# Two interleaved layers, a spectral filter and a long convolution: the last eight units of the convolution's kernel are made in the second part

## The chip, the cores and the metric

One core of one Trainium2 chip runs the whole program. The metric is device time in microseconds (us) of one execution; smaller is better. Engines are called PE (TensorE), DVE (VectorE), ACT (ScalarE), POOL (GpSimd) and SP (SyncE, which here only issues DMAs).

## The reference

Four residual steps on x of 2048 x 512 values: layer A, layer B, layer A, layer B, each on a layer norm of x.

```python
def _A_ref(x, w_r, w_i):                     # S, D = 2048, 512
    X = rfft2(x) * (w_r + 1j * w_i)
    return irfft2(X, s=(S, D))

def _B_ref(u, ...):                          # D = 512 channels, N = 128 states, L = 2048
    P = exp(dt * A * l)                      # complex, D x N x L
    K = einsum("dn,dnl,dn->dl", C, P, dt * B).real
    y = irfft(rfft(u, 2 * L) * rfft(K, 2 * L))[:L]
    return y + u * Dskip

x = x + _A_ref(layernorm(x), ...)
x = x + _B_ref(layernorm(x), ...)
x = x + _A_ref(layernorm(x), ...)
x = x + _B_ref(layernorm(x), ...)
```

Both layers B use the same K, which does not depend on x.

## The kernel before

Transforms are matmuls with cosine and sine tables in several steps. x stays in SBUF as 128 partitions x 16 rows (`s2`) x 512 columns.

**The kernel K** is made in 32 units (`unit_k`) of 16 channels. Four units are a block `b`, eight units a quarter `q` of the channels. For a block, `load_k` loads factors by DMA, and six steps of `exp_k` make magnitudes: two factor matmuls into a PSUM pair (L1194) and one exponential on ACT (L1210) into a buffer `M`. A unit then does this:

- PE: two factor matmuls, the phases, into a PSUM pair `p` (L1194)
- ACT: `c` = phases plus a constant that rounds them (L1224)
- DVE: `s`, the phase's remainder, from `c` and `p` (L1226), and its absolute value into `c` (L1227)
- ACT: sine of `c`, the cosine part (L1229), and of `s` (L1230, written to PSUM `p`)
- DVE: the imaginary half of `E` = sine times magnitude (L1237 and L1238, which read PSUM `p` and SBUF `M`)
- POOL: the real half of `E` = `c` times magnitude (L1241 and L1242)
- PE: 64 small matmuls of `E` (L1254), and DVE two copies of their sums into `KS` (L1265)

After eight units `store_k` sends `KS` to DRAM (`kd`, L1274), and `turn_k` loads it back (L1285), turns it on PE (L812) and sends it, by way of ACT copies (L1301), to DRAM `yk`. For the first half of the channels (units 0 to 15) `spectra_k` makes spectra from `yk` in the first part and stores them in `khat`.

**Layer A** (`forward_a`, `first_a`, `group_a`, `inv_a`) goes in 16 rows, 16 groups of frequencies and 16 inverse rows. After its inverse, `inv_a` adds the result to x on DVE (L792, L794).

**Layer B** works on two halves `e` of the columns. `norm_b` normalises a row of x (for the first layer on DVE, L554; for the second on ACT, L552). `turn_x` turns 32 columns of it (PE L828, and a DVE transpose, L830). Columns 128 to 255 go another way: `forward_b` (PE L812, ACT copies, DMA to DRAM `yd`) and `place_b` (DMA back, L859). Then eight groups `group_b` for each half: PE spectrum of rows (L881), DVE times the spectra of K (L951), POOL sums (L958), PE back (L968), ACT copies (L973). The second half's groups of the first layer load `yk` (L929) and make their spectra of K there; all others load `khat` (L940). `inv_b` (L1019) and `back_b` bring the result to x.

**The order** is made when the program is built: each step is a generator of pieces, a class `Clock` keeps modelled times of engines, buffers and dependences, and a list scheduler emits the piece of the lowest rank among those that are ready. The engines then run that order, each its own instructions strictly one after another. Matmuls at L413 fill PE's modelled idle time. There are two such lists, run one after the other: the **first part** (loads, all of K but the last quarter's turn, the first layer A, the first norms), and the **second part** (the last quarter's turn, first layer B, second layer A, second layer B). No piece of the second part stands ahead of one of the first on any engine. I call the place where they meet the seam. Buffers are rings cut from three big tiles (`wk`, `Y`, `Ya`) anew for each part; PSUM is split in banks by kind, the `a` kind having three pairs in the first part and four in the second.

Of the kernel before, what the change touches and what calls it, by code (L numbers as in the profile page):

```python
# [53 lines left out]
WORK = 16896  # L54
# [143 lines left out]
class Clock:  # L198
# [4 lines left out]
    def __init__(self, net, last=None):  # L203
# [3 lines left out]
        self.pools, self.lands = [], []  # L207
# [231 lines left out]
class Net:  # L439
    def __init__(self, tc, io, ctx):  # L440
# [324 lines left out]
    def inv_a(self, r, s2, st):  # L765
# [21 lines left out]
        nc.tensor.matmul(q, self.RaT, Y4, start=True, stop=True)  # L787
        self.drop(Y4)
# [25 lines left out]
    def norm_b(self, r, s2, st):  # L814

        k = (id(st), s2 // 4, s2 // 2 % 2) if r else (id(st), s2 // 4)
        yield "ACT" if NORMS[2 * r + 1] else "DVE", self.after(k), self.emitted(("group", 1), 16 * r), self.emitted(("inverse", 0), 16)
        self.norm(s2, st, slice(0, 512), self.xn[:, s2])
        self.mark("normed", r, s2 // 4)

    def turn_x(self, r, e, i):

        yield "PE p:a", *(self.after(("normed", r, b), 4) for b in range(4)), self.emitted(("turned", r), 4), self.emitted(("mult", r), PACE[r] * i * e)
        p = self.psum("a")
        o = 256 * e + 32 * i
        for w in range(2):
            rows = slice(64 * w, 64 * w + 64)
            self.nc.tensor.matmul(p[:, 512 * w:512 * w + 512], self.Rf[rows, :], self.xn[rows, :, o:o + 32], start=True, stop=True)  # L828
# [4 lines left out]
    def forward_b(self, r, b):  # L833

        kind = "f" if r else "a"
        ring = "iy" if r else f"t{1 + b // 2}"
# [5 lines left out]
        self.turn_b(self.xn[:, 4 * b:4 * b + 4, 128:256], ps)  # L842
# [137 lines left out]
    def back_b(self, r, e, b):  # L980
# [5 lines left out]
        yield "SP io", self.after(("grouped", r, e), 8), self.emitted(("rows", r, 1), 8)  # L986
# [26 lines left out]
    def inv_b(self, r, e, i):  # L1013
# [3 lines left out]
        yield "DVE wo", self.after(("grouped", r, e), 8), self.emitted(("rows", r, 1), 8), self.emitted(("mult", r), 8 + LATE[r] * (i - first) if not e else 0)  # L1017
# [45 lines left out]
    def load_h(self):  # L1063
        self.oh = self.ring["oh"][0].bitcast(BF)[:96]
# [114 lines left out]
    def load_k(self, b):  # L1179
# [334 lines left out]
```

## Time and profile before

| | before |
|---|---|
| median of 3 runs | 748.66 us (745.71 to 748.88) |
| the profiled execution | 748.11 us |
| its span | 746.3 us |
| PE busy | 624.4 us (84%) |
| DVE busy | 556.4 us (75%) |
| ACT busy | 405.2 us (54%) |
| POOL busy | 279.3 us (37%) |
| DMA | 121.52 MB, mean 163 GB/s |

A profile's row names the line of the kernel, the engine, the operation, output and inputs by the program's names, and the shape. The span runs from the first instruction to the last. An idle time is put down to what ended it. "Busy" PE includes the filling matmuls of L413.

### The profile page before, as it was taken

The page shows a single profiled execution, that of the slowest core. Times are in us where ns is not written, and L with a number is a line of the kernel's source. Part 1 is how long each engine was busy: PE and PEld are TensorE (multiplying, and loading weights), DVE is VectorE, ACT ScalarE, POOL GpSimd, SP SyncE. Part 2 cuts the span into 40 slices and gives each one's busy share as a digit, 9 for nine tenths or more (in the row PEclk, how much of TensorE's full clock was granted, in tenths as well). Part 3 has the DMA queues.
Part 4 walks back from the last instruction along what each step waited for, and adds up shares of the span by engine and source line. Part 5 has one row for each costly group of instructions (what it writes and reads, how often), then busy time and mean ns, then how long its engine had stood idle before and what let it go on. Part 6 is the DMA issues. An engine that isn't in the chain of part 4 may idle for free. (4 is left out here: it accounts for less than half of the span.)

```text
span 746.3 us, 19649 instructions
## 1 busy us (share of the span) xinstructions
PE 624.4 (84%) x8138; PEld 390.1 (52%) x8138; DVE 556.4 (75%) x923; ACT 405.2 (54%) x654; POOL 279.3 (37%) x275
## 2 busy tenths in 40 slices
PE   3799888888989888878688899889887799898883
PEld 3778566556755434344333446477766544444241
DVE  5977578657685877589569899786798488798664
ACT  5677889887788886784223431176544145322220
POOL 4283255534353533051035452075444100056440
PEclk9999999999999999989899999899999999999997
DMA  9433412642432973544997766400658000578967
GB/s 334 138 106 106 133 51 86 164 128 84 115 114 62 310 203 94 183 142 113 310 320 237 247 208 227 163 1 1 219 194 274 2 2 1 198 244 260 351 184 206
DMA packets 109785, 121.52 MB, mean 163 GB/s; under 512 B 5916, under 2 KB 90912, under 8 KB 109568
## 3 DMA queue, kind: packets, MB, share of 16 engines
q1 hardware_dynamic: 67760, 90.90, 38.3%
q10 hardware_dynamic: 41936, 29.37, 12.4%
q8 instruction: 64, 1.05, 0.6%
q14 instruction: 25, 0.20, 0.1%
HBM read 80.53 MB, written 39.71 MB: 161 GB/s over the span
## 5 line engine op out<-in xcount | busy, mean ns | idle before, releaser
L958 POOL TENSOR_TENSOR apart<-wk 128x512 f32<-128x512 f32 x64 | 79.8, 1274 | 167.7 <-DVE wk L951 154.8
L1241 POOL TENSOR_TENSOR Y<-wk,Y 128x1024 f32<-128x1024 f32 x32 | 64.8, 2023 | 113.4 <-issue 68.0
L951 DVE TENSOR_TENSOR wk<-ps,wk 128x1024 f32<-128x1024 f32 x64 | 74.5, 1220 | 15.0 <-PE ps L881 5.3
L973 ACT COPY Y<-ps 128x512 f32<-128x512 f32 x64 | 34.4, 589 | 92.9 <-PE ps L968 82.9
L413 PEld LDWEIGHTS ps<-cRa,cRb 128*128 128x128 f32 x550 | 64.3, 193 | 18.4 <-issue 13.1
L413 PE MATMUL ps<-cRa,cRb 128*128 128x128 f32 x550 | 69.3, 281 | 3.3 <-DMA cRb<-in_cRb_dram 3.3
L779 PE MATMUL ps<-cDaT,apart 128*32 128x256 f32 x256 | 60.8, 388 | 4.5 <-DVE x L794 4.5
L1226 DVE SCALAR_TENSOR_TENSOR wk<-wk,ps 128x1024 f32<-128x1024 f32 x32 | 38.9, 1215 | 16.5 <-ACT wk L1224 16.4
L830 DVE STREAM_TRANSPOSE Y<-ps 128x1024 f32<-128x1024 f32 x24 | 44.4, 1930 | 6.3 <-PE ps L828 6.2
L968 PE MATMUL ps<-apart,wk 32*64 32x256 f32 x1024 | 43.1, 398 | 6.6 <-POOL apart L958 5.7
L1210 ACT ACTIVATE Y<-ps 128x1024 f32<-128x1024 f32 x48 | 46.0, 1028 | 4.8 <-PE ps L1194 4.1
L1194 PE MATMUL ps<-wk,Y 96*128 96x512 bf16 x128 | 40.5, 394 | 9.2 <-ACT Y L1210 4.6
L597 PE MATMUL ps<-cRa,wk 128*128 128x256 f32 x128 | 35.6, 403 | 14.9 <-POOL wk L579 13.6
L1254 PEld LDWEIGHTS ps<-Y 128*32 128x32 f32 x2048 | 34.8, 121 | 25.0 <-issue 19.2
L1254 PE MATMUL ps<-Y 128*32 128x64 f32 x2048 | 39.8, 237 | 9.6 <-ACT wk L783 3.5
L579 POOL TENSOR_TENSOR wk<-wk 128x256 f32<-128x256 f32 x32 | 26.2, 819 | 55.3 <-ACT wk L552 26.5
L1237 DVE TENSOR_TENSOR Y<-ps,Y 128x1024 f32<-128x1024 f32 x32 | 39.0, 1218 | 9.2 <-ACT ps L1230 9.2
L779 PEld LDWEIGHTS ps<-cDaT,apart 128*32 128x32 f32 x256 | 26.7, 111 | 34.9 <-DVE x L794 8.1
L881 PE MATMUL ps<-Y,wk 64*32 64x256 f32 x1024 | 36.3, 392 | 9.4 <-ACT Y L973 4.5
L1229 ACT ACTIVATE wk<-wk,quarter 128x1024 f32<-128x1024 f32 x32 | 36.7, 1147 | 13.2 <-DVE wk L1227 11.2
L1224 ACT ACTIVATE wk<-ps,magic 128x1024 f32<-128x1024 f32 x32 | 35.4, 1123 | 9.7 <-PE ps L1194 3.6
L1019 DVE STREAM_TRANSPOSE Ya<-Y 128x1024 f32<-128x1024 f32 x16 | 34.1, 2154 | 7.3 <-ACT Y L973 7.3
(205 smaller groups left out, 1512.4 us busy)
## 6 DMA issues: line engine op xcount, KB each, us to landing
wk<-khat SPq DMA_DIRECT2D x24, 512.0 KB
yk<-wk ACTq DMA_DIRECT2D x32, 256.0 KB
Ya<-vd SPq DMA_DIRECT2D x16, 512.0 KB
Y<-in_W_dram SPq DMA_DIRECT2D x12, 515.0 KB
x<-in_cPa_dram SPq DMA_DIRECT2D x16, 384.0 KB
Y<-in_cGa_dram SPq DMA_DIRECT2D x12, 384.0 KB
x<-in_W_dram SPq DMA_DIRECT2D x16, 258.0 KB
x<-in_A_x_dram SPq DMA_DIRECT2D x8, 512.0 KB
```

Of the source, the lines that this page charges most:

```text
L413: self.net.nc.tensor.matmul(bank[:, :128], self.net.Rb, self.net.Ra[:, 1], start=True, stop=True)
L779: nc.tensor.matmul(p[32 * i:32 * i + 32, o:o + 256], self.folded(r, i)[:, b, s2].rearrange("p g m -> p (g m)"), self.DaT[:, b, :], start=b ...
L830: self.nc.vector.transpose(self.place[e][:, :, 32 * i:32 * i + 32].rearrange("p k d -> p d k"), p.rearrange("p (w s d) -> p d s w", w=2, s ...
L951: nc.vector.tensor_tensor(t[c], x, kh[:, :, ::-1, :] if c else kh, op=OP.mult)
L958: nc.gpsimd.tensor_tensor(Z[:, :, c], t[0][:, :, c], t[1][:, :, c], op=op)
L968: nc.tensor.matmul(v[j][64 * a:64 * a + 64, h], gi[o:o + 32, j, 4 + 2 * c:6 + 2 * c, :].rearrange("p a m -> p (a m)"), Z[o:o + 32, j, c, : ...
L1194: self.nc.tensor.matmul(p, f[:, c:c + 128], self.oh[:k, o:o + 512], start=True, stop=True)
L1210: nc.scalar.activation(m[:, :, 1024:] if i == 2 else m[:, i, :1024], p.rearrange("p (i m) -> p i m", i=2) if i == 2 else p, AF.Exp)
L1226: nc.vector.scalar_tensor_tensor(s, c, MAGIC, p, op0=OP.subtract, op1=OP.subtract)
L1237: nc.vector.tensor_tensor(E[:, 1, :1024], p, m[:, :1024], op=OP.mult)
L1241: nc.gpsimd.tensor_tensor(E[:, 0, :1024], c, m[:, :1024], op=OP.mult)
L1254: nc.tensor.matmul(pk[32 * j:32 * j + 32, 64 * e:64 * e + 64], E1[:, r, i, :], E2[:, r, i], start=r == 0, stop=r == 1)
```

## The change

The line numbers of the changed file are about 22 to 29 higher in the functions named here (L1237 becomes L1266, L1238 L1267, L1226 L1255, L1227 L1257, L1265 L1294, L554 L576, L830 L852, L951 L973, L940 L962, L859 L881, L812 L835, L881 L903, L1274 L1303, L1285 L1313).

- Blocks 0 to 5 (units 0 to 23) stay in the first part. Of blocks 6 and 7 only the factor loads and the six exponentials of block 6 are made there; their eight units, the exponentials of block 7, the store and the turn of the last quarter go to the second part, by ranks beside the first layer B's first half.
- The first layer's `norm_b` is done by halves of the columns: half 0 in the first part, half 1 in the second. Half 0 lies in `wk`, half 1 in `Ya`. The second layer's norm is also issued as two halves. Half 0 waits until all of layer A's inverses are emitted.
- The sine of `s` is written over `s` in SBUF instead of into PSUM `p`; `p` is given back after L1226's counterpart, and DVE multiplies two operands in SBUF.
- Buffers move: factors, `KS` and some of the units' buffers are carried over the seam; `khat` gets three buffers instead of four for the first layer (five as before for the second).
- Groups' loads of `khat` and tables behind the first two wait in the emitted order until the four sends of `forward_b` are out (`HOLD`).
- `back_b` and `inv_b` wait in the emitted order for the last quarter's turn. The planner's test whether two accesses meet compares ranges of columns. Some ranks change.

```diff
-RANK = -4, 0.25, 4, 1.1, 24, 0.5, 25, 0.4
+EXPS = 1
+BLOCKS, RANK2 = 6, (-10, 0.6, 0)
+RANK = -4, 0.25, -2, 1.3, 18, 0.6, 20, 0.5
...
-HOLD = 0
+HOLD = 4
...
-    def norm_b(self, r, s2, st):
-
+    def norm_b(self, r, s2, st, e=None):
...
-        self.norm(s2, st, slice(0, 512), self.xn[:, s2])
-        self.mark("normed", r, s2 // 4)
+        for i in (0, 1) if e is None else (e,):
+            self.norm(s2, st, slice(256 * i, 256 * i + 256), self.xn[r][i][:, s2])
+            self.mark("normed", r, i, s2 // 4)
...
         nc.vector.scalar_tensor_tensor(s, c, MAGIC, p, op0=OP.subtract, op1=OP.subtract)
+        self.drop(p)
         nc.vector.tensor_scalar(c.bitcast(U32), s.bitcast(U32), 0x7fffffff, None, op0=OP.bitwise_and)
         yield "ACT"
         nc.scalar.activation(c, c, AF.Sin, scale=-TURN, bias=self.quarter)
-        nc.scalar.activation(p, s, AF.Sin, scale=-TURN)
-        self.drop(s)
+        nc.scalar.activation(s, s, AF.Sin, scale=-TURN)
...
-        nc.vector.tensor_tensor(E[:, 1, :1024], p, m[:, :1024], op=OP.mult)
-        nc.vector.scalar_tensor_tensor(E[:, 1, 1024:], p[:, 512:], -1.0, m[:, 1024:], op0=OP.mult, op1=OP.mult)
-        self.drop(p)
+        nc.vector.tensor_tensor(E[:, 1, :1024], s, m[:, :1024], op=OP.mult)
+        nc.vector.scalar_tensor_tensor(E[:, 1, 1024:], s[:, 512:], -1.0, m[:, 1024:], op0=OP.mult, op1=OP.mult)
+        self.drop(s)
...
-        for b in range(8):
-            yield 4 * b - 2, self.load_k(b)
-            for n in range(6):
-                yield 4 * b - 1, self.exp_k(b, n, M)
...
+        yield from self.units(range(BLOCKS), M, KS)
+        for b in range(BLOCKS, min(8, BLOCKS + 2)):
+            yield 4 * b - 2, self.load_k(b, True)
+            for n in range(6 if b < BLOCKS + EXPS else 0):
+                yield 4 * b - 1, self.exp_k(b, n, M, True)
...
-        for i in range(4):
-            yield 3 * i, self.turn_k(3, i)
+        yield from self.units(range(BLOCKS, 8), *self.live, RANK2[0] - 4 * RANK2[1] * BLOCKS, RANK2[1], RANK2[2])
+        for s2 in range(16):
+            yield -10, self.norm_b(0, s2, sb, 1)
         yield from layer_b(0, 0)
```

**DVE at the seam.** In the program before, DVE goes from the last norms (L554) to the row turns (L830), the last quarter's skip term (L1292) and the groups' products (L951):

```order
L554 TENSOR_SCALAR Ya<-x,mv,rs 128x512 x6
L830 STREAM_TRANSPOSE Y<-ps 128x32x32 x5
L1292 TENSOR_TENSOR wk<-wk 1x4x32
L951 TENSOR_TENSOR wk<-ps,wk 128x1024 x2
L830 STREAM_TRANSPOSE Y<-ps 128x32x32
L951 TENSOR_TENSOR wk<-ps,wk 128x1024 x4
```

In the changed program, from the last norms of half 0 (L576), units (L1255 to L1267 and L1294) stand ahead of the row turns (L852) and between them:

```order
L576 TENSOR_SCALAR wk<-x,mv,rs 128x256 x11
L1255 SCALAR_TENSOR_TENSOR wk<-Y,ps 128x1024
L1257 TENSOR_SCALAR Y<-wk 128x1024
L1255 SCALAR_TENSOR_TENSOR wk<-Y,ps 128x1024
L1257 TENSOR_SCALAR Y<-wk 128x1024
L1266 TENSOR_TENSOR Ya<-wk,Y 128x1024
L1267 SCALAR_TENSOR_TENSOR Ya<-wk,Y 128x512
L852 STREAM_TRANSPOSE Y<-ps 128x32x32 x2
L1294 COPY wk<-ps 128x4x32 x2
L1266 TENSOR_TENSOR Ya<-wk,Y 128x1024
```

The first products of a group come after four units' products; the other four units stand between groups; behind the last come 16 half norms and the eight row turns of half 1. L1266 and L1267 read no `ps`.

**SP at the seam.** Before, the last quarter's store (L1274, to `kd`) is the first of the second part's transfers, and its reloads (L1285) stand between the loads of tables (L911), of `khat` (L940) and the place loads (L859):

```order
L1274 DMA kd_97<-wk 64x2x512 x4
L911 DMA wk<-in_cGb_dram 128x512
L940 DMA wk<-khat 128x4x256 x2
L1285 DMA wk<-kd_97 128x4x128 x2
L940 DMA wk<-khat 128x4x256 x2
L911 DMA wk<-in_cGb_dram 128x512
L1289 DMA wk<-in_B_Dskip_dram 1x128
L1285 DMA wk<-kd_97 128x4x128
L859 DMA Y<-yd_106 128x4x128 x4
```

In the changed program the same place has no `kd_97`; from the place loads (L881) on:

```order
L881 DMA Y<-yd_106 128x4x128 x4
L933 DMA wk<-in_cGb_dram 128x512
L881 DMA Y<-yd_106 128x4x128 x4
L933 DMA wk<-in_cGb_dram 128x512 x4
L962 DMA wk<-khat 128x4x256 x5
L1303 DMA kd_97<-wk 64x2x512 x4
L1313 DMA Ya<-kd_97 128x4x128 x2
```

The last quarter's store and reloads now stand behind all eight loads of `khat` for the first half. The third quarter's store and reloads stand ahead of the seam.

**PE at the last quarter's turn.** Before, after the row turns (L828) PE has the first turn of K (L812, from `wk`), fill and the groups:

```order
L828 MATMUL ps<-Ya,cRf 128x512 x10
L812 MATMUL ps<-wk,cRb 128x512 x2
L413 MATMUL ps<-cRa,cRb 128x128 x11
L812 MATMUL ps<-wk,cRb 128x512 x4
L881 MATMUL ps<-Y,wk 32x256 x16
```

In the changed program it stands behind the units, all eight spectra of the first half's groups and six of their eight ways back, in turn with the row turns of half 1 (L850):

```order
L850 MATMUL ps<-Ya,cRf 128x512 x2
L835 MATMUL ps<-Ya,cRb 128x512 x2
L850 MATMUL ps<-Ya,cRf 128x512 x2
L835 MATMUL ps<-Ya,cRb 128x512 x2
L850 MATMUL ps<-Ya,cRf 128x512 x2
```

A row turn behind a turn of K waits on PE until that turn's reload has landed.

More of the change, by code (lines that the diff above doesn't have):

```diff
@@ L216, in tile @@
         assert slots, name
-        slots.sort()
-        t, i = slots.pop(0)
+        t, i = min(s for s in slots if (name, s[1]) not in self.closed)
+        slots.remove((t, i))
         tile = make(i)
@@ L266, in boxes @@
         step = min([a for a, _ in rest], default=1)
-        return [(p, max(1, s // width), n, low * size, step * size, (low + span) * size) for low in lows]
+        inner = sum(a * (b - 1) for a, b in rest[1:]) + 1
+        far = rest[0][0] if rest and rest[0][0] > inner else 0
+        return [(p, max(1, s // width), n, low * size, step * size, (low + span) * size, far * size, (inner if far else span) * size) for low in lows]
     @staticmethod
     def meet(a, b):
-        for p, s, n, o, t, e in a:
-            for p2, s2, n2, o2, t2, e2 in b:
+        for p, s, n, o, t, e, f, w in a:
+            for p2, s2, n2, o2, t2, e2, f2, w2 in b:
+                m = max(f, f2)
+                if m and (f == f2 or not min(f, f2)) and o % m + w <= m and o2 % m + w2 <= m and (o % m + w <= o2 % m or o2 % m + w2 <= o % m):
+                    continue
                 if e <= o2 or e2 <= o or p + s * (n - 1) < p2 or p2 + s2 * (n2 - 1) < p:
@@ L393, in time @@
                 if slots is not None:
+                    slots = [s for s in slots if (name, s[1]) not in self.closed]
                     if len(slots) < names.count(name):
@@ L985, in back_b @@
         s = slice(n * b, n * b + n)
-        yield "SP io", self.after(("grouped", r, e), 8), self.emitted(("rows", r, 1), 8)
+        yield "SP io", self.after(("grouped", r, e), 8), self.emitted(("rows", r, 1), 8), self.emitted(("turn", 1), 8)
         y = self.w("io", [128, n, 2, d.stop - d.start])
@@ L1016, in inv_b @@
         first = OUT[r][e] // 32
-        yield "DVE wo", self.after(("grouped", r, e), 8), self.emitted(("rows", r, 1), 8), self.emitted(("mult", r), 8 + LATE[r] * (i - first) if not e else 0)
+        yield "DVE wo", self.after(("grouped", r, e), 8), self.emitted(("rows", r, 1), 8), self.emitted(("turn", 1), 8), self.emitted(("mult", r), 8 + LATE[r] * (i - first) if not e else 0)
         y = self.w("wo", [128, 32, 32])
@@ L1298, in turn_k @@
         for w in range(2):
-            yield "ACT iy" if last else "ACT yh"
-            y = self.w("iy" if last else "yh", [128, 4, 128])
+            yield "ACT yh"
+            y = self.w("yh", [128, 4, 128])
             nc.scalar.copy(y.rearrange("p s (j d) -> p s j d", j=4), p[w].rearrange("p (j s d) -> p s j d", j=4, s=4))
```

103 lines of the change are left out of this document (68 added, 35 removed).

## The prediction

> **What bounds the kernel now.** I read the stages first, since the change moves work from one to another. Each row gives a stretch of the span in us and its length, then the busy us (and instructions) of PE, PE's weight loads, DVE, ACT and POOL, the granted TensorE clock, the DMA share and GB/s.
>
> ```profile
> core 0 of [0], span 746.3 us
> 78.00:242.60 164.60, 145.60 (x2060) 98.98 (x2064) 113.64 (x181) 139.10 (x168) 73.70 (x56) 0.97 0.35 105
> 242.60:348.70 106.10, 89.46 (x1576) 43.61 (x1564) 81.40 (x151) 79.69 (x98) 34.23 (x22) 0.94 0.55 170
> 348.70:375.00 26.30, 17.91 (x88) 9.32 (x89) 16.74 (x25) 7.51 (x13) 0.00 (x0) 0.87 0.97 297
> 375.00:411.00 36.00, 29.62 (x564) 14.03 (x563) 29.94 (x22) 10.32 (x20) 17.43 (x14) 1.00 0.89 273
> 411.00:463.00 52.00, 48.06 (x912) 27.42 (x913) 48.30 (x51) 17.82 (x27) 22.66 (x18) 1.00 0.70 229
> ```
>
> Stage 1 (78 to 242.6, units beside the first layer A's groups) has PE busy 88% and ACT 85%. Stage 2 (to 348.7, the rest of the units beside the inverse of layer A) has PE at 84%, DVE at 77%. Then the second part begins, and its limit is another: from 411 to 463 DVE is busy 93%. Over 348.7 to 463 DVE works 16.74 + 29.94 + 48.30 = 95.0 of 114.3 us, and its 19.3 idle us lie mostly in one hole at the seam. The next rows show that hole: start, length, instruction, and in brackets the idle time ahead of it and what ended it.
>
> ```profile
> 348.06 3.43 SPq L1274 DMA_DIRECT2D kd<-wk  x3
> 358.64 1.92 DVE L830 STREAM_TRANSPOSE Y<-ps 128x1024 f32<-128x1024 f32 x1 [2.19 <-PE ps L828]
> 359.35 0.57 SPq L1285 DMA_DIRECT2D wk<-kd  x1
> 367.81 2.08 PE L812 MATMUL ps<-wk,cRb 64*128 64x512 f32 x4 [5.88 <-DMA wk<-kd]
> 371.61 0.28 DVE L1292 TENSOR_TENSOR wk<-wk 1x128 f32<-1x128 f32 x1 [4.20 <-DMA wk<-in_B_Dskip_dram]
> 376.24 2.36 DVE L951 TENSOR_TENSOR wk<-ps,wk 128x1024 f32<-128x1024 f32 x2 [4.35 <-PE ps L881]
> ```
>
> The second part is idle at its start behind DMA (share 0.97) and behind DVE ever after. So ACT is free there (35.65 of 114.3 us: 7.51 + 10.32 + 17.82), and DVE is not. A unit needs both, so its price per engine decides. Columns: busy us and mean ns, then idle before.
>
> ```profile
> L1210 ACT ACTIVATE Y<-ps 128x1024 f32<-128x1024 f32 x48 | 46.0, 1028 | 4.8 <-PE ps L1194 4.1 <-ACT wk L901 0.4
> L1194 PE MATMUL ps<-wk,Y 96*128 96x512 bf16 x128 | 40.5, 394 | 9.2 <-ACT Y L1210 4.6 <-DVE Y L1237 2.4 <-DMA Y<-spe 1.0
> L1237 DVE TENSOR_TENSOR Y<-ps,Y 128x1024 f32<-128x1024 f32 x32 | 39.0, 1218 | 9.2 <-ACT ps L1230 9.2
> L1226 DVE SCALAR_TENSOR_TENSOR wk<-wk,ps 128x1024 f32<-128x1024 f32 x32 | 38.9, 1215 | 16.5 <-ACT wk L1224 16.4
> L1229 ACT ACTIVATE wk<-wk,quarter 128x1024 f32<-128x1024 f32 x32 | 36.7, 1147 | 13.2 <-DVE wk L1227 11.2 <-DVE wk L1265 0.5 <-DVE wk L1226 0.4
> L1242 POOL TENSOR_TENSOR Y<-wk,Y 128x512 f32<-128x512 f32 x32 | 36.2, 1131 | 0.0
> L1224 ACT ACTIVATE wk<-ps,magic 128x1024 f32<-128x1024 f32 x32 | 35.4, 1123 | 9.7 <-PE ps L1194 3.6 <-DMA khat<-wk 2.2 <-POOL x L739 1.5
> L1230 ACT ACTIVATE ps<-wk 128x1024 f32<-128x1024 f32 x32 | 32.3, 1008 | 0.0
> L1227 DVE TENSOR_SCALAR wk<-wk 128x1024 uint32<-128x1024 uint32 x32 | 24.2, 755 | 2.4
> L1238 DVE SCALAR_TENSOR_TENSOR Y<-ps,Y 128x512 f32<-128x512 f32 x32 | 21.8, 681 | 0.0
> L1265 DVE COPY wk<-ps 128x128 f32<-128x128 f32 x64 | 19.2, 377 | 18.7 <-PE ps L1254 17.1 <-ACT wk L1301 1.6
> L1229 ACT ACT_TABLE_LOAD x10 | 12.8, 1283 | 1.4 <-ACT wk L1301 1.3
> ```
>
> **The change, part by part.** One unit costs DVE 1.215 + 0.755 + 1.218 + 0.681 + 2 x 0.377 = 4.62 us and ACT 1.123 + 1.147 + 1.008 = 3.28 us, besides six exponentials of 1.03 us and some table loads of 1.28 us for each four units. For PE the rows of its products by stage give the price.
>
> ```profile
> 78.00:242.60 164.60, 24.91 (x1344) 21.54 (x1344) 0.97 0.35 105
> 242.60:348.70 106.10, 14.94 (x716) 13.28 (x704) 0.94 0.55 170
> ```
>
> That is 21 units of 64 matmuls in stage 1, 1.19 us each, and 11 in stage 2, 1.36 us each. In the changed order 18 units stand ahead of the first inverse, 6 beside the inverses and 8 behind the seam.
>
> *The sine in SBUF, and the price of a shared port.* The second sine is now written to SBUF, not PSUM. On ACT I take L1229's time instead of L1230's: 0.14 us a unit, hidden, for ACT is not first in any stage once units leave. DVE then multiplies two SBUF operands where it had one in PSUM. By L1237's row this costs nothing. But rows of the same trace say more: a DVE instruction on SBUF alone that meets a POOL instruction waits for that to end.
>
> ```profile
> 180.08 0.42 DVE L741 TENSOR_TENSOR x<-x 128x257 f32<-128x257 f32 x1
> 105.45 0.59 DVE L741 TENSOR_TENSOR x<-x 128x257 f32<-128x257 f32 x1
> 103.75 2.01 POOL L1241 TENSOR_TENSOR Y<-wk,Y 128x1024 f32<-128x1024 f32 x1
> 181.73 1.86 DVE L1227 TENSOR_SCALAR wk<-wk 128x1024 uint32<-128x1024 uint32 x1
> 181.05 2.00 POOL L1241 TENSOR_TENSOR Y<-wk,Y 128x1024 f32<-128x1024 f32 x1 [2.85 <-issue]
> 183.00 1.54 POOL L1242 TENSOR_TENSOR Y<-wk,Y 128x512 f32<-128x512 f32 x1
> 92.12 1.22 DVE L1237 TENSOR_TENSOR Y<-ps,Y 128x1024 f32<-128x1024 f32 x1
> 90.54 2.08 POOL L1241 TENSOR_TENSOR Y<-wk,Y 128x1024 f32<-128x1024 f32 x1 [0.74 <-ACT wk L1229]
> 330.61 1.19 DVE L1237 TENSOR_TENSOR Y<-ps,Y 128x1024 f32<-128x1024 f32 x1
> 329.28 2.00 POOL L1241 TENSOR_TENSOR Y<-wk,Y 128x1024 f32<-128x1024 f32 x1 [0.61 <-POOL Y L1242]
> ```
>
> L741, two SBUF operands, takes 0.42 us alone; begun inside POOL's L1241, which ends at 105.76, it ends at 106.04. L1227, begun inside L1241, ends 0.54 us after it, and meanwhile POOL's L1242 takes 1.54 us instead of 1.13. L1237 as it stands, with PSUM, runs through the same neighbour at 1.22 us (92.12 and 330.61, the first and the last of 22 units of 32 that begin inside L1241, with on average 1.02 us of it still to go). As an SBUF instruction it would wait that out, and L1238 would find L1242 (1.13 us) in its way: 22/32 x (1.02 + 1.13), about 1.5 us a unit; bounds 0 (DVE always late or POOL always late) and 2.2. In the stages where DVE is behind its queue it reaches L1237 later, when POOL may be done, so there I take 1.0.
>
> The Trainium skill, GPSIMD Engine Reference, section Key points, says that GpSimd shares its SBUF interfaces with VectorE and contends with VectorE instructions in a two-port mode or with two SBUF inputs. L741 and L1227 agree with it and L1237 in PSUM is just the case that it exempts; by L1237's row the changed kernel would come to 751 us (second rival), by the page's rule to the forecast. Nothing else in the sum hangs on the page.
>
> *Stage 1* loses 3 units and 6 exponentials. PE: 3 x 1.19 and 18 factor matmuls of at most 0.39 us, 10.7 us of 145.6; at the same busy share that is 10.7 x 164.6/145.6 = 12 us. ACT would allow more (3 x 3.28 + 6 x 1.03 = 16 us). DVE falls by 13.9 to 99.7 and gains 18 x 1.5 = 27: 127 of 153 us, third in the race but close, and each unit's product reaches PE about 1.4 us later. I charge 5 us (0 to 17). Stage 1: **-7**.
>
> *Stage 2* loses 5 units. PE: 5 x 1.36 + 10 x 0.39 = 10.7 us, to 78.8; at its present share 93 us, at the full share of the second layer's inverse, which stands alone, 79 us.
>
> ```profile
> 589.50:634.60 45.10, 45.10 (x547) 20.79 (x546) 34.10 (x89) 21.23 (x39) 0.00 (x0) 1.00 0.01 2
> L552 ACT ACTIVATE Ya<-x,nb,rs 128x512 f32<-128x512 f32 x16 | 12.2, 806 | 0.4 <-DVE nb L543 0.4
> ```
>
> I take 92, nearer to the present share, because six units, eight spectra and the turns of the third quarter still cut in: **-14**. The early release of a unit's PSUM pair (after L1226's counterpart, not after L1238's) counts here and in stage 1; no long wait in the trace is for it, so it gets no term.
>
> *The seam to 463.* The norms on DVE are cut into halves, 27 of which stand behind the last inverse instead of these 12 whole ones:
>
> ```profile
> L554 DVE TENSOR_SCALAR Ya<-x,mv,rs 128x512 f32<-128x512 f32 x12 | 5.7, 537 | 0.0
> ```
>
> A half costs between 0.27 and 0.54 us; at 0.33, near the lower end since the work halves, 27 cost 9, that is 3 more. DVE adds 8 x 4.62 = 37.0 us of units, 8 x 1.0 = 8 of waiting for POOL, and these 3. 95 + 48 = 143 us of DVE work. The units fill the hole: of 19.3 idle us I leave 8. So 151 us instead of 114.3: **+37**. ACT (35.65 and 8 x 3.42, 6 exponentials and about four table loads: 74 us), PE (95.6 to about 117) and POOL (40 to 65) fit under it. The floor is no wait and no idle time, 95 + 40 = 135, **+21**; the ceiling is under the third rival. Everything in this term follows from the stretch being DVE's.
>
> The seam's DMA changes too: the last quarter's store and its reload stand behind the first half's khat loads, and the place loads go earlier. What the hole holds is work now, so this earns nothing more than those 11 idle us.
>
> *After 463* the order is nearly the same. ACT's 16 norms of L552 become 32 halves; between 0 and one more full set of 806 ns, but beside an inverse whose ACT is half idle; the last ones stand ahead of the turns: **+1**.
>
> Sum against the profiled execution's own 748.11 us (its span and 1.8 outside; 0.55 below the median of the runs shown): -7 - 14 + 37 + 1 = +17, **765 us**.
>
> **Rivals.** *The first part shrinks fully, and the kernel is faster.* If stage 1 runs at a PE share of 95% (134.9/0.95 = 142, -23) since PSUM pairs come free early and POOL's wait is hidden, and stage 2 at the 100% of the second inverse (-27), then -50 + 37 + 1 = -12: 736 us. It decides from the point where the first part gives back over 38 us. For it: DVE has room there, ACT loses 32 us. Against: no stage with units shows a PE share above 88%.
>
> *No price for the port.* If POOL and DVE do not meet in the new order, stage 1 gives 12, stage 2 15 (1 more), and the second part costs 29 (37 - 8): +3 with the last term, 751 us. Against: the two products of a unit hang on the same sines, 1 us apart.
>
> *The last quarter's way through DRAM shows.* Its store (348.06 now), reload (359.35 issued, landed 367.81) and yk writes now start behind the last unit, and PE has a turn of it between each pair of row turns. Ahead of the first of these turns DVE has one or two groups of 2.36 us and 16 half norms, some 10 us, against 20 us from store to first turn today (in a DMA stretch that is 0.97 full, which the new place is not). If PE waits 10 us there, and the port costs its whole 1.5 (+4) and hides nothing in stage 1 (+12 more), 765 + 26 is about 790 us.
>
> That the change does not move the units is excluded: the new order shows them.
>
> **How the numbers follow.** Forecast 0.50 (755 to 778 by itself), the faster rival 0.22, no port price 0.16, the exposed way 0.12. About 0.5% is what a measurement of this kernel can tell from no change: 745 to 752. Faster 0.24 (the first rival and a little of the second), same 0.14, slower 0.62. The range runs from 742, which leaves out the deeper half of the first rival, to 788.
>
> **What would show it.** Units' SBUF products on DVE at a mean of over 1.8 us instead of 1.218; the first inverse beginning at about 235 and the last ending near 328; from there to the second layer's first matmuls about 150 us with DVE over 90% busy. It is wrong if the mean stays near 1.2, if the first part ends before 310, or if the second part's stretch grows by less than 25 us.

## The result and the profile after

The changed kernel takes 816.53 us (median of 4 runs, 809.96 to 818.85) against 748.56 us before (4 runs): a ratio of 1.090 (95% interval 1.083 to 1.098). It is 68 us slower, where 17 were forecast, and outside the range. The profiled execution took 809.96 us, its span 808.2; against the profiled execution before, the spans differ by 61.9 us. Times and ratios here and below leave out executions that fell into a slower state of the chip.

The stages of the changed kernel follow, with the columns as before: stretch, length, then the busy us and instructions of PE, weight loads, DVE, ACT and POOL, granted clock, DMA share and GB/s. The first two rows after the heading are stages 1 and 2; the next four are the second part's beginning, and the last is the stretch that answers to 348.7 to 463 before.

```profile
core 0 of [0], span 808.2 us
78.00:260.20 182.20, 146.69 (x1819) 97.46 (x1822) 143.66 (x164) 122.06 (x151) 94.37 (x50) 0.88 0.32 93
260.20:355.50 95.30, 77.85 (x1231) 36.77 (x1230) 71.68 (x117) 58.90 (x77) 28.73 (x12) 0.95 0.61 190
355.50:384.00 28.50, 24.16 (x220) 14.28 (x220) 23.76 (x37) 15.91 (x22) 8.39 (x4) 0.83 0.72 232
384.00:444.00 60.00, 45.10 (x871) 27.25 (x878) 58.68 (x53) 30.62 (x35) 44.69 (x24) 0.74 0.28 82
444.00:471.00 27.00, 20.50 (x162) 9.36 (x160) 22.50 (x25) 6.94 (x13) 4.98 (x4) 0.94 0.55 150
471.00:529.00 58.00, 49.86 (x924) 27.87 (x920) 50.83 (x53) 18.95 (x27) 20.22 (x16) 1.00 0.78 257
355.50:525.70 170.20, 137.16 (x2145) 76.83 (x2146) 152.48 (x163) 72.41 (x95) 78.27 (x48) 0.87 0.56 176
```

Stage 1 has 18 units instead of 21 and yet is longer by 17.7 us: DVE is busy 143.7 us for 18 units, where it was 113.6 for 21. Stage 2 is 10.8 us shorter. From 384 to 444, where most of the moved units run, DVE is busy 98% and the granted clock is 0.74.

I compare all kernels by four places on PE's timeline: the first factor matmul, the first and the last inverse of the first layer A, and the first matmul of the second layer A. "The rest" goes from there to PE's last matmul. Lengths in us:

| | stage 1 | stage 2 | seam to second layer A | the rest |
|---|---|---|---|---|
| before | 164.2 | 106.1 | 137.4 | 250.4 |
| after | 181.9 | 95.3 | 192.7 | 250.2 |
| difference | +17.7 | -10.8 | +55.3 | -0.2 |

The groups that answer to the price list of before: busy us and mean ns, then idle before. `Ya` is the buffer of the units behind the seam. The first row is POOL's first product in the kernel before; the others are of the changed kernel.

```profile
L1241 POOL TENSOR_TENSOR Y<-wk,Y 128x1024 f32<-128x1024 f32 x32 | 64.8, 2023 | 113.4 <-issue 68.0 <-ACT wk L1229 44.3 <-POOL Y L1242 1.0
L1270 POOL TENSOR_TENSOR Y<-wk,Y 128x1024 f32<-128x1024 f32 x24 | 62.6, 2609 | 94.1 <-ACT wk L1259 53.2 <-issue 39.9 <-POOL Y L1271 1.0
L1266 DVE TENSOR_TENSOR Y<-wk,Y 128x1024 f32<-128x1024 f32 x24 | 59.4, 2473 | 2.7 <-ACT wk L1260 2.5
L1271 POOL TENSOR_TENSOR Y<-wk,Y 128x512 f32<-128x512 f32 x24 | 50.3, 2096 | 0.0
L1267 DVE SCALAR_TENSOR_TENSOR Y<-wk,Y 128x512 f32<-128x512 f32 x24 | 39.9, 1662 | 0.0
L1257 DVE TENSOR_SCALAR wk<-wk 128x1024 uint32<-128x1024 uint32 x24 | 21.0, 873 | 1.5
L1266 DVE TENSOR_TENSOR Ya<-wk,Y 128x1024 f32<-128x1024 f32 x8 | 18.4, 2302 | 0.5 <-ACT wk L1260 0.5
L1267 DVE SCALAR_TENSOR_TENSOR Ya<-wk,Y 128x512 f32<-128x512 f32 x8 | 14.0, 1753 | 0.0
```

DVE's two products of a unit went from 1218 + 681 to 2473 + 1662 ns, 2.24 us more; behind the seam they are 2.16 more. POOL pays too: 2023 + 1131 became 2609 + 2096 ns, 1.55 more. One unit on POOL's and DVE's timelines (start, length, instruction, idle ahead):

```profile
217.79 2.37 POOL L1270 TENSOR_TENSOR Y<-wk,Y 128x1024 f32<-128x1024 f32 x1 [3.72 <-issue]
220.10 2.26 POOL L1271 TENSOR_TENSOR Y<-wk,Y 128x512 f32<-128x512 f32 x1
218.64 2.60 DVE L1266 TENSOR_TENSOR Y<-wk,Y 128x1024 f32<-128x1024 f32 x1 [1.66 <-ACT wk L1260]
221.16 1.75 DVE L1267 SCALAR_TENSOR_TENSOR Y<-wk,Y 128x512 f32<-128x512 f32 x1
```

The four ends stand in turn: POOL 220.16, DVE 221.24 (1.08 later), POOL 222.36 (1.12 later), DVE 222.91 (0.55 later). Each gap is nearly the later instruction's uncontended time: 1.22 for L1266, 1.13 for L1271, 0.68 for L1267. The two engines take turns, and each works only while the other stands. In 23 of the 32 units the four ends come in this order, with gaps of about 1.08, 1.12 and 0.55 us; in the others DVE came later or met POOL in another order.

The seam, as before by start, length, instruction and idle time ahead:

```profile
366.32 1.22 DVE L1255 SCALAR_TENSOR_TENSOR wk<-Y,ps 128x1024 f32<-128x1024 f32 x1 [3.80 <-ACT Y L1253]
440.94 3.36 SPq L1303 DMA_DIRECT2D kd<-wk  x4
448.46 1.24 SPq L1313 DMA_DIRECT2D Ya<-kd  x2
452.66 2.08 PE L835 MATMUL ps<-Ya,cRb 64*128 64x512 f32 x4 [3.67 <-DMA Ya<-kd]
452.71 0.28 DVE L1320 TENSOR_TENSOR Ya<-Ya,wk 1x128 f32<-1x128 f32 x1 [2.64 <-DMA wk<-in_B_Dskip_dram]
456.34 1.91 DVE L852 STREAM_TRANSPOSE Y<-ps 128x1024 f32<-128x1024 f32 x1 [1.52 <-PE ps L850]
480.33 2.35 DVE L973 TENSOR_TENSOR wk<-ps,wk 128x1024 f32<-128x1024 f32 x2 [3.06 <-PE ps L903]
```

The last quarter goes out at 440.94 and its first turn begins at 452.66, 12 us later. PE waits 3.67 us for the reload and DVE 2.64 and 1.52.

### The profile page after: what moved, and what is told of

It is laid out like the page before. It is cut to its first block, busy times and chain, and to the rows that moved or that the text cites. A ratio compares the mean times of both kernels' runs of the same rounds, so it can differ in the third digit from the quotient of the medians.

```text
span 808.2 us, 19726 instructions
## 1 busy us (share of the span) xinstructions
PE 654.3 (81%) x8158; PEld 410.5 (51%) x8158; DVE 632.6 (78%) x939; ACT 408.5 (51%) x668; POOL 332.6 (41%) x275
## 5 line engine op out<-in xcount | busy, mean ns | idle before, releaser
L980 POOL TENSOR_TENSOR apart<-wk 128x512 f32<-128x512 f32 x64 | 82.3, 1310 | 149.9 <-DVE wk L973 144.4
L1270 POOL TENSOR_TENSOR Y<-wk,Y 128x1024 f32<-128x1024 f32 x24 | 62.6, 2609 | 94.1 <-ACT wk L1259 53.2
L973 DVE TENSOR_TENSOR wk<-ps,wk 128x1024 f32<-128x1024 f32 x64 | 74.9, 1225 | 11.3 <-PE ps L903 4.9
L433 PEld LDWEIGHTS ps<-cRa,cRb 128*128 128x128 f32 x570 | 71.0, 203 | 18.1 <-issue 12.1
L433 PE MATMUL ps<-cRa,cRb 128*128 128x128 f32 x570 | 76.7, 292 | 2.9 <-DMA cRb<-in_cRb_dram 2.9
L1220 PE MATMUL ps<-oh,wk 96*128 96x512 bf16 (+1 forms) x160 | 55.2, 428 | 14.4 <-ACT Y L1239 5.6
L1266 DVE TENSOR_TENSOR Y<-wk,Y 128x1024 f32<-128x1024 f32 x24 | 59.4, 2473 | 2.7 <-ACT wk L1260 2.5
L1271 POOL TENSOR_TENSOR Y<-wk,Y 128x512 f32<-128x512 f32 x24 | 50.3, 2096 | 0.0
L852 DVE STREAM_TRANSPOSE Y<-ps 128x1024 f32<-128x1024 f32 x24 | 44.5, 1931 | 7.3 <-PE ps L850 7.3
L1283 PE MATMUL ps<-Y 128*32 128x64 f32 x1536 | 34.7, 251 | 18.2 <-DVE wk L1294 6.2
L903 PE MATMUL ps<-Y,wk 64*32 64x256 f32 x1024 | 38.3, 414 | 10.1 <-ACT Y L995 5.1
L1283 PEld LDWEIGHTS ps<-Y 128*32 128x32 f32 x1536 | 29.0, 130 | 30.1 <-issue 13.5
L1270 POOL TENSOR_TENSOR Ya<-Y 128x1024 f32<-128x1024 f32 x8 | 20.3, 2540 | 55.8 <-ACT Y L1259 43.7
L1255 DVE SCALAR_TENSOR_TENSOR wk<-wk,ps 128x1024 f32<-128x1024 f32 x24 | 29.0, 1210 | 14.0 <-ACT wk L1253 13.9
L1267 DVE SCALAR_TENSOR_TENSOR Y<-wk,Y 128x512 f32<-128x512 f32 x24 | 39.9, 1662 | 0.0
```

The costliest lines, as they stand in the source:

```text
L433: self.net.nc.tensor.matmul(bank[:, :128], self.net.Rb, self.net.Ra[:, 1], start=True, stop=True)
L852: self.nc.vector.transpose(self.place[e][:, :, 32 * i:32 * i + 32].rearrange("p k d -> p d k"), p.rearrange("p (w s d) -> p d s w", w=2, s ...
L903: self.nc.tensor.matmul(X[j][o:o + 32, 256 * c:256 * c + 256], G[i, j, 2 * h + c, :], y[j][i, h, :], start=True, stop=True)
L973: nc.vector.tensor_tensor(t[c], x, kh[:, :, ::-1, :] if c else kh, op=OP.mult)
L980: nc.gpsimd.tensor_tensor(Z[:, :, c], t[0][:, :, c], t[1][:, :, c], op=op)
L1220: self.nc.tensor.matmul(p, f[:, c:c + 128], self.oh[:k, o:o + 512], start=True, stop=True)
```

## The experiments

Where an expectation says that an order is held, the list scheduler repeats the choices of an earlier build, so that the engines' order stays and only the edit acts. "Replanned" means that the planner chose anew. "Early" is the release of PSUM `p` ahead of the sines, which the change brought with the sine in SBUF.

### Is it the port?

**sine_psum**: the changed kernel with the sine back in PSUM, `p` held as before, replanned.

```diff
-        self.drop(p)
...
-        nc.scalar.activation(s, s, AF.Sin, scale=-TURN)
+        nc.scalar.activation(p, s, AF.Sin, scale=-TURN)
+        self.drop(s)
...
-        nc.vector.tensor_tensor(E[:, 1, :1024], s, m[:, :1024], op=OP.mult)
+        nc.vector.tensor_tensor(E[:, 1, :1024], p, m[:, :1024], op=OP.mult)
...
```

> The changed kernel with one part undone: the second sine goes to PSUM again and the PSUM pair is held until DVE's two products have read it; the planner orders anew. Port theory (DVE's products on two SBUF operands and POOL's products shut each other out, and that is nearly all of what was not forecast): DVE's products come back to 1.22 and 0.68 us, POOL's to 2.0 and 1.1; the stage of units before the first inverse falls from 182 to about 152 us, the seam's stretch from 170 to about 150; total 755 to 775 us. Plan theory (the units behind the seam and the new order cost the time by themselves): total above 795. Clock theory (the lower granted clock, 0.92 against 0.96, costs it): total above 790 with the clock still near 0.92.

781.98 us, ratio 1.0445 (1.0388 to 1.0503): 34.6 of the 68 us went. That lies between what the port theory and the plan theory gave, so it decides between neither. And this is a new plan, with POOL laid beside another instruction of DVE:

```profile
L1256 DVE TENSOR_SCALAR wk<-wk 128x1024 uint32<-128x1024 uint32 x24 | 27.3, 1136 | 1.6
```

The absolute value, on SBUF alone, now takes 1136 ns (755 before). Part of the clash was moved, not removed.

**before_sbuf_sine**: the kernel before, its order held, with only the sine in SBUF and `p` still held to the end of the products. The sine gets a third buffer, for which a table (`oh`) gets a place of its own in SBUF.

```diff
-        nc.scalar.activation(p, s, AF.Sin, scale=-TURN)
-        self.drop(s)
+        nc.scalar.activation(s, s, AF.Sin, scale=-TURN)
...
-        nc.vector.tensor_tensor(E[:, 1, :1024], p, m[:, :1024], op=OP.mult)
+        nc.vector.tensor_tensor(E[:, 1, :1024], s, m[:, :1024], op=OP.mult)
...
-        self.drop(p)
+        self.drop(s, p)
...
```

> The kernel before, with its emitted order held word for word, and one part of the change alone: the second sine goes to SBUF (a third buffer for it) and DVE's products read two SBUF operands; the PSUM pair is held as before. Port theory: DVE's products take 2.3 to 2.5 and 1.6 to 1.7 us, POOL's 2.6 and 2.0; 32 units times about 2.2 us on DVE, partly beside its idle time: 785 to 810 us. Plan theory: within 5 us of 748. Clock theory: the time grows only if the clock falls.

789.55 us, 1.0544 (1.0491 to 1.0597): 41 us from this edit alone, with nothing moved. Its groups and its first stage:

```profile
L1243 DVE TENSOR_TENSOR Y<-wk,Y 128x1024 f32<-128x1024 f32 x32 | 66.4, 2074 | 6.8 <-ACT wk L1237 6.8
L1244 DVE SCALAR_TENSOR_TENSOR Y<-wk,Y 128x512 f32<-128x512 f32 x32 | 49.6, 1550 | 0.0
```

```profile
78.90:270.20 191.30, 156.08 (x2056) 104.69 (x2060) 156.19 (x180) 140.11 (x168) 95.80 (x56) 0.92 0.31 92
```

The products are 1.73 us a unit longer, 55 us in 32 units, and 41 of them (74%) show in the time. Stage 1 takes 191.3 us and stage 2 118.5, against 164.2 and 106.1: the price falls where I had called DVE third in the race.

**after_pool_cut** and its control **before_pool_cut**: the changed order, and the order before, held; POOL's products of a unit do 16 columns. This leaves the real half of K unmade.

```diff
-        nc.gpsimd.tensor_tensor(E[:, 0, :1024], c, m[:, :1024], op=OP.mult)
+        nc.gpsimd.tensor_tensor(E[:, 0, :16], c[:, :16], m[:, :16], op=OP.mult)
...
```

> The changed kernel's emitted order held word for word, but POOL makes only 16 columns of each of its two products (the rest of the real half of E is left out), so POOL hardly uses the port beside the units. Port theory: DVE's products fall to 1.1 to 1.25 and 0.6 to 0.7 us, 2.2 us a unit; total 755 to 780 us. Plan theory: above 800. Clock theory: near 815, unless the clock rises.

> Control: the kernel before, its emitted order held word for word, with the same cut of POOL's products. There DVE's products read PSUM and never met POOL at the port. Port theory: little, 735 to 748 us, since POOL's time was seldom last. If POOL's own time (not the port) were what the cut takes away in the changed kernel, this one falls by as much, 35 us or more.

762.04 us, 1.0172 (1.0124 to 1.0221), so 54 of the 68 us are gone; the control took 747.22, 0.9982 (0.9955 to 1.0009), so in the order before POOL's products themselves are worth nothing that can be told. DVE's product, two operands in SBUF but no POOL beside it, and stage 1 and the seam's stretch of the changed order without POOL:

```profile
L1273 DVE TENSOR_TENSOR Y<-wk,Y 128x1024 f32<-128x1024 f32 x24 | 29.9, 1247 | 6.4 <-ACT wk L1267 6.0
```

```profile
78.80:232.40 153.60, 136.89 (x1819) 92.27 (x1819) 100.14 (x164) 120.93 (x151) 21.39 (x50) 0.93 0.39 110
316.90:473.20 156.30, 129.26 (x2146) 74.05 (x2145) 135.82 (x162) 72.11 (x95) 48.15 (x48) 0.91 0.61 192
```

The SBUF operand costs DVE next to nothing (1247 against 1218 ns); the neighbour does. Without POOL, stage 1 takes 153.6 us instead of 181.9, stage 2 84.6 instead of 95.3, and seam to second layer A 179.8 instead of 192.7: the port is worth 28, 11 and 13 us there. Part of the 28 is on PE's own timeline: for the same 1819 matmuls PE is busy 146.7 us at a granted clock of 0.88, and 136.9 at 0.93 without POOL. So PE is busy about 10 us longer and idle about 19 longer. No run separates what the lower clock costs by itself from what the waits cost.

**before_sbuf_early**: the kernel before with the change's whole unit, early release included, replanned.

```diff
         nc.vector.scalar_tensor_tensor(s, c, MAGIC, p, op0=OP.subtract, op1=OP.subtract)
+        self.drop(p)
...
-        nc.scalar.activation(p, s, AF.Sin, scale=-TURN)
-        self.drop(s)
+        nc.scalar.activation(s, s, AF.Sin, scale=-TURN)
...
```

> The kernel before with the change's unit entire (sine in SBUF, and the PSUM pair given back early), ordered anew by its planner, all units in the first part. With the pair held the same sine cost 41 us. If the early release pays as it should for the planner, 5 to 15 us come back: 775 to 785 us. If PSUM was not short: 785 to 795.

797.82 us, 1.0632 (1.0564 to 1.0699), 8 us above before_sbuf_sine and above both ranges expected. The early release gains nothing that shows, in this plan.

### Is it DVE's length or POOL's?

Both engines take turns at the port, so both grow longer. Two kernels on the code before, where the sine is in PSUM and DVE's products do not wait for POOL's, lengthen one at a time.

**dve_twice**:

```diff
-        nc.vector.tensor_tensor(E[:, 1, :1024], p, m[:, :1024], op=OP.mult)
-        nc.vector.scalar_tensor_tensor(E[:, 1, 1024:], p[:, 512:], -1.0, m[:, 1024:], op0=OP.mult, op1=OP.mult)
+        for _ in range(2):
+            nc.vector.tensor_tensor(E[:, 1, :1024], p, m[:, :1024], op=OP.mult)
+            nc.vector.scalar_tensor_tensor(E[:, 1, 1024:], p[:, 512:], -1.0, m[:, 1024:], op0=OP.mult, op1=OP.mult)
```

> The kernel before, emitted order held word for word, sine in PSUM, but DVE makes its two products of each unit twice: 1.9 us more of DVE a unit with POOL left alone. (The SBUF sine in this order gave DVE 1.7 and POOL 0.9 us more a unit, and 41 us in all.) If it is DVE's longer products that show: 25 to 45 us more, 775 to 795. If it is POOL's longer products: under 12 us more.

**pool_twice**: the second product of POOL twice in the same way.

> The kernel before, order held, sine in PSUM, but POOL makes the second of its two products twice: 1.13 us more of POOL a unit, DVE left alone. If POOL's length shows: 15 to 30 us more. If DVE's: under 8 us, 748 to 757.

dve_twice took 793.38 us, 1.0599 (1.0552 to 1.0645): +43.5 for 32 x 1.90 = 61 us of DVE. pool_twice took 763.32, 1.0195 (1.0135 to 1.0256): +13.5 for 32 x 1.13 = 36 us of POOL. Stage 1 of each:

```profile
78.50:269.70 191.20, 159.53 (x2060) 105.19 (x2064) 149.19 (x223) 139.12 (x167) 74.02 (x56) 0.90 0.31 92
```

```profile
79.00:258.20 179.20, 153.65 (x2053) 103.07 (x2056) 119.12 (x181) 139.76 (x168) 98.29 (x77) 0.92 0.32 97
```

Longer DVE products, with the sine in PSUM, give the same stage 1 as the SBUF sine, 191.2 and 191.3 us. POOL's length shows too, about half as much for its us; 763.32 lies between the two ranges expected. POOL was not lengthened quite alone, though: DVE's absolute value met it more often (mean 872 ns, 755 before), and DVE was busy 119.1 us in stage 1 instead of 113.6. So DVE's length counts more, and POOL's share in the changed kernel, where POOL grew by 1.55 us a unit, is not isolated.

DVE is busy only 78% of dve_twice's stage 1. Where its length shows nevertheless, the waits say: engine and line that waited, for what, us in total, times, longest. First stage 1 of dve_twice and of pool_twice, on PE, then the kernel before.

```profile
PE ps L1201 <- DVE Y L1245: 18.3, 14, 2.9
```

```profile
PE ps L1262 <- POOL Y L1250: 13.5, 12, 2.3
```

```profile
PE ps L1194 <- DVE Y L1237: 2.4, 3, 1.0
ACT wk L1229 <- DVE wk L1227: 6.6, 4, 2.9
DVE wk L1226 <- ACT wk L1224: 14.7, 6, 4.5
```

In before, ACT waits for DVE and DVE for ACT, in a loop; with longer products PE's wait for them grows from 2.4 to 18.3 us. That wait is for the PSUM pair `p`, which DVE's products still read in this kernel. The changed kernel gives `p` back earlier, and there the waits are others. Its stage 1, with the last row from after_pool_cut, whose L1266 and L1264 are the changed kernel's L1259 and L1257:

```profile
ACT wk L1259 <- DVE wk L1257: 20.7, 5, 6.3
DVE wk L1255 <- ACT wk L1253: 13.9, 6, 3.8
PE ps L1283 <- DVE Y L1267: 4.5, 6, 3.2
PE ps L1283 <- DVE wk L1294: 4.1, 2, 3.2
```

```profile
ACT wk L1266 <- DVE wk L1264: 4.7, 3, 2.0
```

ACT's wait for DVE is 20.7 us with the port and 4.7 in the same order without it, and PE waits 4.5 us for DVE's products and 4.1 for its copies. DVE's idle time in that stage, 38.5 us, is mostly waiting for other engines, longest for ACT (13.9 for L1253 alone). That these waits, in a loop, are what makes DVE's length show is argued from the rows; no run removed one of them.

### Is the seam DVE's alone?

**seam_products_cut**: after_pool_cut, with DVE's products of units 24 to 31 also cut to 16 columns.

```diff
-        nc.vector.tensor_tensor(E[:, 1, :1024], s, m[:, :1024], op=OP.mult)
...
+        n = 16 if u >= 4 * BLOCKS else 1024
...
+        nc.vector.tensor_tensor(E[:, 1, :n], s[:, :n], m[:, :n], op=OP.mult)
...
```

> The changed kernel's emitted order held word for word, POOL's products cut to 16 columns as in the earlier run (762 us), and now DVE's two products of the eight units of the second part cut to 16 columns too (the rest of E is left out): 8 x about 1.7 us of DVE work less, all at the seam. DVE theory (DVE's work sets the stretch behind the seam): 13 us less, 747 to 752 us. Chain theory (the stretch is set by waits from engine to engine, ACT's sines, the last quarter's way): 3 us less or none, 758 to 763.

758.05 us, 1.0113 (1.0072 to 1.0154), 4 us below after_pool_cut. The stretch that answers to 348.7 to 463 before:

```profile
318.20:468.10 149.90, 123.77 (x2145) 69.82 (x2146) 121.74 (x162) 71.77 (x95) 44.18 (x48) 0.95 0.64 200
```

DVE's work fell by 135.8 - 121.7 = 14.1 us and the stretch by 156.3 - 149.9 = 6.4. So the stretch is not DVE's alone, although DVE was busy 87% in it: DVE's idle time went from 20.5 to 28.2 us.

**copies_on_act**: the changed order held, the two copies of each unit behind the seam (L1294) moved from DVE to ACT.

```diff
-            nc.vector.tensor_copy(KS[u // 8][:, l, o:o + 4].rearrange("p l e -> p e l"), k[:, :, h])
+            (nc.scalar.copy if u >= 4 * BLOCKS else nc.vector.tensor_copy)(KS[u // 8][:, l, o:o + 4].rearrange("p l e -> p e l"), k[:, :, h])
```

> The changed kernel's emitted order held, but the eight units of the second part copy their sums into KS on ACT (16 copies of 0.37 us), not on DVE; ACT is busy 45% there. DVE theory: DVE loses 6 us of work in a stretch that it bounds, 808 to 812 us against 816. If the seam is bound by something else (the planner's waits, DMA): within 2 us of 816, or slower by what ACT's copies hold up there.

811.98 us, 1.0824 (1.075 to 1.0897), 4.5 us below the changed kernel, with intervals that overlap. The median stands at the edge of what the DVE theory gave, but in the profile the stretch is 168.6 us with 148.8 of DVE work, against 170.2 with 152.5: 3.7 us less work, 1.6 us less time. The run decides nothing by itself.

### The other rivals

**no_reload_wait**: the changed order held; the last quarter's turn reads the third quarter's place in DRAM, which is long ready.

```diff
-        kd = self.kd[q].rearrange("w a j m -> (w a) j m")
+        kd = self.kd[min(q, 2)].rearrange("w a j m -> (w a) j m")
```

> The changed kernel's emitted order held word for word, but the last quarter's turn reloads the third quarter's rows (so its values are wrong), which have long been stored: nothing waits for the last store to land. Exposed-way theory (the last quarter's way through DRAM shows behind the last unit): the 7 to 10 us in which DVE idles around that turn go, 804 to 809 us against 816. DVE theory (the stretch is DVE's alone and the wait only moves): within 3 us of 816.

815.6 us, 1.084 (1.0783 to 1.0896). The skip term's row, and the stretch of the seam:

```profile
453.43 0.27 DVE L1327 TENSOR_TENSOR Ya<-Ya,wk 1x128 f32<-1x128 f32 x1
```

```profile
358.90:527.90 169.00, 135.46 (x2146) 75.02 (x2146) 152.35 (x162) 72.43 (x95) 78.29 (x48) 0.89 0.57 178
```

The wait of 2.64 us is gone and the stretch is 1.2 us shorter. The way through DRAM is not where the changed kernel loses its time.

**fill_twice**: the changed order held, each group of filling matmuls twice as long, to raise the granted clock. The order of the engines' other work is the same.

> The changed kernel's emitted order held, with each run of filling matmuls twice as long (285 become 570 calls, about 30 us of PE, put where the planner took PE to be idle). Clock theory (the granted clock of 0.92 against 0.96 costs time by itself): the clock rises to 0.94 or more and the time falls by 5 us or more. Port and DVE theory: PE is not last in those stretches, the clock is an effect; the time stays within 5 us or grows by up to 15 where fill runs past the wait it covers.

842.53 us, 1.1182 (1.1115 to 1.125). The granted clock was 0.944 to 0.946, where the changed kernel's was 0.916 to 0.922, and the time rose by 26 us, more than the 15 allowed for. The added matmuls take PE's time themselves, so the run shows that a clock raised in this way does not pay; it does not show what the lower clock costs.

**before_hold**: the kernel before with the change's `HOLD = 4`.

> The kernel before with one small part of the change alone: loads of khat and of tables behind the first two are emitted after the four sends of forward_b (HOLD = 4). It aims at the hole of 18 us on DVE at the seam. If the hole is DMA's order: the first group starts up to 5 us earlier, 743 to 748 us. If the hole is DMA's volume: no difference, within 0.3% of before.

753.42 us, 1.0037 (1.0001 to 1.0072), no gain.

### What the moving itself costs

Three kernels with the sine in PSUM differ in how many units move.

**psum_four**: sine_psum with `BLOCKS = 7`, `EXPS = 1`: four units behind the seam instead of eight.

> The changed kernel with its sine in PSUM again (the earlier run, 782 us), and only the last four units behind the seam instead of eight (BLOCKS = 7). DVE theory: each unit moved saves about 2 us in the first part and costs about 5 behind the seam, so half the units give back half of the loss: 762 to 770 us. If the loss is the plan's (halved norms, buffers, ranks), not the units': 778 to 784.

**psum_none**: sine_psum with `BLOCKS = 8`: none behind it.

> The same with no unit behind the seam (BLOCKS = 8): the sine in PSUM, and of the change only the halved norms, the order of loads, the buffers and the ranks are left. DVE theory: near the kernel before, 743 to 757 us. Plan theory: above 770.

**psum_unmoved**: the changed code with the sine in PSUM, no units moved, the old ranks (`TURN_X` among them) and no `HOLD`, and the last quarter's turn in the second part as before. What is left of the change is the halved norms, the buffers and the planner's test.

```diff
-BLOCKS, RANK2 = 6, (-10, 0.6, 0)
-RANK = -4, 0.25, -2, 1.3, 18, 0.6, 20, 0.5
+BLOCKS, RANK2 = 8, (-10, 0.6, 0)
+RANK = -4, 0.25, 4, 1.1, 24, 0.5, 25, 0.4
...
-TURN_X = 2, 8, 0.5
+TURN_X = 8, 8, 2
...
-HOLD = 4
+HOLD = 0
...
+        for i in range(4):
+            yield 3 * i, self.turn_k(3, i)
```

> The changed kernel's code with the sine in PSUM, no unit behind the seam (BLOCKS = 8), the last quarter's turn in the second part as before, and the ranks, TURN_X and HOLD of before: of the change only the halved norms, the buffers and the planner's tests are left. If these cost nothing: 745 to 757 us, and the 33 us of the run with eight moved units and the sine in PSUM are the moving's and its ranks'. If they cost: above 765.

| | us | ratio (interval) | stage 1 | stage 2 | seam to second layer A |
|---|---|---|---|---|---|
| sine_psum (8 moved) | 781.98 | 1.0445 (1.0388 to 1.0503) | 162.2 | 92.8 | 181.6 |
| psum_four | 772.83 | 1.032 (1.0231 to 1.0409) | 162.4 | 104.9 | 162.1 |
| psum_none | 798.62 | 1.0628 (1.0543 to 1.0712) | 164.0 | 111.5 | 179.5 |
| psum_unmoved | 762.56 | 1.0169 (1.0107 to 1.0231) | 168.4 | 108.3 | 142.9 |

psum_four and psum_unmoved came out between the ranges expected of them, and psum_none, at 798.62, far above the "near the kernel before" of the DVE theory. psum_none does not isolate the move. Its last quarter's way stands at the end of the first part and stalls the seam, as its own timeline shows:

```profile
382.32 3.40 SPq L1303 DMA_DIRECT2D kd<-wk  x4
393.17 4.92 PE L835 MATMUL ps<-wk,cRb 64*128 64x512 f32 x12 [5.78 <-DMA wk<-kd]
419.14 1.92 DVE L852 STREAM_TRANSPOSE Y<-ps 128x1024 f32<-128x1024 f32 x1 [18.52 <-PE ps L850]
```

DVE stands 18.52 us there for a row turn that is queued on PE behind the turns of K. From psum_four to sine_psum, four units moved save 12.3 us in the first part and cost 19.5 at the seam: 3.1 a unit saved and 4.9 paid. psum_unmoved is 13 us above the kernel before with nothing moved; so 19 of sine_psum's 33 are the moved units and the ranks. Neither number is free of the port: in psum_unmoved the absolute value takes 824 ns and POOL's products 2415 and 1307, above their 755, 2023 and 1131 of before. These are different plans, and the split between them is rough.

## Why the prediction was wrong

**Right.** It is slower, and most of it by a price on two SBUF operands beside POOL. Of the signs named, DVE's products at a mean above 1.8 us came (2.47 and 2.30); the first inverse at 260 us and the last at 355 did not fit 235 and 328. With that price taken away (after_pool_cut) the terms of stage 1 and of DVE's work stand: stage 1 is 10.6 us shorter (12 worked out from PE's share), and DVE's work from the seam on is 135.8 us, where 95 + 37 + 3 = 135 was forecast. The Trainium skill's rule (GPSIMD Engine Reference, Key points: contention of GpSimd with VectorE instructions that have two SBUF inputs) agrees with L1266 at 2473 ns beside POOL and 1247 without it. That section gives no size. The reload's wait was small, and from the second layer A on nothing changed (-0.2, where +1 was forecast for all after 463).

**The step that failed: "I charge 5 us (0 to 17)".** The port was worth 28.3 us in stage 1, 10.7 in stage 2 and 12.9 behind the seam, 52 in all by these stages and 54 by the medians, where I had 5 + 1 + 8 = 14. (The rest was 3 us longer without POOL's products, so the two profiled spans differ by 48.) Two errors made it so. The smaller is the price of a unit: 1.5 us, and 1.0 behind the seam because "DVE is behind its queue" there, against 2.24 and 2.16. The sum had both waits in it, but took them for 22 units of 32, those whose product begins inside POOL's first one, and gave the others nothing. In the same trace 9 more begin inside POOL's second product, and in the changed kernel 30 of 32 run beside POOL's. With 1.02 + 1.13 = 2.15 us for every unit the price would have been nearly right; in the order before, held, it was 1.73. The larger error is what a unit's price does to the time. I set DVE's 127 us beside a stage of 153, called it "third in the race" and took the difference as room. In the run 18 x 2.24 = 40 us of added DVE work made stage 1 longer by 28. dve_twice shows the same without two SBUF operands: 43.5 of 61 us come out in the time, with DVE busy 78% of stage 1. The waits suggest why: DVE's idle time in stage 1 is mostly waiting for ACT and PE, which wait for DVE in turn, so it was not room.

**The second: "of 19.3 idle us I leave 8" and "Everything in this term follows from the stretch being DVE's".** The stretch is 170.2 us for 152.5 of DVE work: 17.7 idle, and 20.5 without POOL's products. The units did not fill the hole down to 8 us; there are new waits, such as the 3.80 us for ACT's L1253. seam_products_cut gave 6.4 us for 14.1 us less of DVE. Without the port, seam to second layer A grew by 42.4 us, where my sum without it was 29. That it is a chain through several engines is argued from this run and the waits; no run removed one link.

**The rivals.** "No price for the port" is settled: after_pool_cut came to 762 us, not 751, since the seam cost 13 us more, the rest 2 and stage 1 1, and stage 2 gave 6 more than that sum had. "The first part shrinks fully" did not happen; but without the port the first part gave 32 us (10.6 + 21.5), nearer to its 38 than I had thought. "The last quarter's way through DRAM shows" falls with no_reload_wait.

**Of the 68 us**, then, about 54 belong to the port, with the lower clock and the waits that follow from it, and about 14 to the rest of the change, from the changed order with and without POOL's products. What stays open is how those 14 divide between the moved units and the halved norms, buffers and planner's test: psum_unmoved gives 13 to the latter in another plan, and the two cannot both be subtracted. No kernel here beats the one before.

## What to carry to other kernels

An engine's busy share is not its room: before adding work to an engine that is busy 70%, look at who waits for whom, and if the engines wait for it in a loop, charge most of the work: here 43.5 of 61 us and 41 of 55. Where two engines meet at a shared port, price both as taking turns for their whole common length, for every pair that runs side by side, and look which operand in PSUM keeps them apart now. Test such a price by moving the one operand in the old order, before anything is moved with it.

## What was not expected of the hardware

- DVE and POOL instructions on SBUF alternated whole: the ends stand about 1.08, 1.12 and 0.55 us apart in 23 of 32 units, each gap near an instruction's uncontended time, and both engines grew longer (DVE 1218 to 2473 ns, POOL's second product 1131 to 2096).
- The absolute value, an instruction with one input in SBUF, was caught too: 1136 ns in sine_psum, against 755 before.
- Doubled filling matmuls went with a granted clock of about 0.945 instead of 0.922, and with 26 us more.
- For the same 1819 matmuls of stage 1 PE was busy 146.7 us at a granted clock of 0.88 and 136.9 at 0.93.
